# A written-out engine order for windowed attention and a two-layer block: uncast transposes for one pair, halved first-layer steps, and a new order of all steps

## The chip, the cores and the metric

The kernel runs on one core of one Trainium2 chip. The metric is device time in microseconds (us) from start to end of one execution. TensorE (PE in the profile) does the matrix products and transposes, VectorE (DVE) and ScalarE (ACT) empty PSUM and do the elementwise work, GpSimd (POOL) issues nearly all loads and does a few copies, SyncE (SP) issues stores, transposing DMAs and two loads. PSUM has eight banks, numbered 0 to 7.

## The reference

```python
B, H, S, D = q.shape                                   # 8, 8, 576, 64
scores = (1 / sqrt(D)) * q @ k^T                       # per batch and head
rel = pos[:, None] - pos[None, :]
scores = where((rel >= 0) & (rel < 64), scores, -1e9)  # causal window of 64
attn = softmax(scores)
x = (attn @ v).transpose(0, 2, 1, 3).reshape(4608, 512)
h = x @ w_in                                           # 512 -> 2048
out = (h - tanh(h)) @ w_out                            # 2048 -> 512, float32
```

## The kernel before

All products run on bf16 operands with float32 sums. The 4608 tokens are cut into nine chunks of 512 for the two dense layers; a batch has 576 tokens, nine windows of 64. The eight heads of a batch are handled in four pairs; pair g stands for batch g // 4, and pairs 0 to 3 are batch 0.

The whole kernel is one list of short words, `PLAN`, which `play` runs from left to right. Each word is a step (a small function) with its numbers and sometimes an engine (p POOL, a ACT, v DVE, s SP). There is no scheduler at run time: each engine does its own steps in the order of the words, waits for the data of each, and holds back everything behind it while it waits. The order of the words is therefore the order of every queue. The words that matter here:

- Loads. `lk.g`, `lq.g` load k and q of a pair (a cast to bf16 happens on the way when POOL issues them; pair 0 comes over SP as float32). `LV.b.i` loads v rows of a batch in blocks of 128 tokens (block 4 is the last 64), `lv.b.pr.half` and `lt.b` do the same by head and for the tail. `wi.i` (three) and `wo.i` (four) load the weights; `wi.2` is twice as large. `lr`, `qr` load k and q of batches 3 to 7, `tk`, `tq` transpose them by DMA.
- `ck.g`, `cq.g` copy a pair's rows into an order in which six transposes do (`tr`, L253). Without that copy `tr` takes twelve transposes of half the width straight from the loaded tile (L249). Before, pairs 2 and 3 do without; pairs 0, 1 and 4 to 11 have the copy.
- `Fp.g.bank`, `Ep.g.bank` are the transposes of k and q on PE; `Fc`, `Ec`, `Ea`, `Eb` move the result from PSUM to SBUF on the engine named.
- `Rp.g.part.bank` are the scores of a pair (for pairs 0 to 3 in two parts over two banks with the mask added by PE, L281 and L286; from pair 4 on in three parts of three matmuls, L292), `Rx` the exponentials on ACT, `M` the mask by product on DVE.
- `Z.b` (and `za`, `zb` by pair) copies v rows across partitions. `P.g`, `PP.g` are the products with v, `D`, `DS`, `DH`, `DR`, `DN` the division by the row sum on DVE into `xs`.
- `Xp.b.half.part.bank` transposes `xs` on PE, `Xc` moves it into `x_chunk`; half 0 holds pairs 0 and 1 of the batch, half 1 pairs 2 and 3. `Y` does the same by DMA for later batches.
- `H.c.m` is a first-layer step (`hp_mm`, L437: four matmuls of 512 columns, contraction 4 x 128), `A.c.m` its tanh on ACT (L445), `G.c.m` the subtraction on DVE (L451), `W.c.s.part` four of the sixteen matmuls of one output tile of the second layer (L480, and L473 for the last), `O` the copy out of PSUM and the store. For chunk 0 the steps H.0.m take the banks 0, 1, 2 in turn, so a step waits for the G of the step three places before it. Two of the four contraction slices of a step belong to half 0 and two to half 1 of `x_chunk`.
- `U.n` are n matmuls on a zero tile `warm` that feed nothing (L220); `i`, `h`, `n`, `u`, `mt`, `mq`, `mv`, `mk`, `mz` make constants and pads.

Of the kernel before, what the change touches and what calls it, by code (L numbers as in the profile page):

```python
# [15 lines left out]
def kernel(  # L16
# [491 lines left out]
    def subtract(c, m, s=None):
# [14 lines left out]
        H=first_layer, A=tanh, G=subtract, W=yp_mm, O=y_out)  # L523

    def play(script):
# [25 lines left out]
        Fc.9.3.a W.0.3.0 Rx.8.1.4 DN.6.0 DN.6.2 W.0.2.0 W.0.2.3 cq.10.a Rp.9.2.4 lr.3.2 Rx.9.2.4 LV.2.4 lr.4.0
        qr.3.3 W.0.3.1 Xp.1.1.0.3 qr.4.1 qr.3.1 Xc.1.1.0.3.a Rp.9.1.4 W.0.3.2 O.0.3.a W.0.2.2 M.8 Z.2 lr.3.4
        Xp.1.1.1.3 W.0.2.1 Xc.1.1.1.3.a LV.3.3 H.1.0 O.0.2.v Ep.10.3 A.1.0 Rx.9.1.4 tq.3.3 Eb.10.3.v H.1.1 H.1.2
        ck.11.v G.1.0 Ea.10.3.a Fp.10.3 Rp.9.0.4 A.1.1 H.1.3 A.1.2 qr.3.4 qr.3.0 lr.3.3 Fc.10.3.a lr.3.0 A.1.3
        qr.4.3 Rx.9.0.4 G.1.1 G.1.2 H.1.4 H.1.5 tq.3.0 qr.4.4 G.1.3 A.1.4 G.1.4 Fp.11.3 lr.3.1 lr.4.1 Rp.10.1.4
        mk M.9 A.1.5 Rx.10.1.4 cq.11.a H.1.6 H.1.7 G.1.5 Fc.11.3.a A.1.6 PP.8 G.1.6 DR.8 A.1.7 Rp.10.2.4 G.1.7
        Ep.11.3 Rx.10.2.4 Eb.11.3.a DN.8.0 LV.3.2 DN.8.2 H.1.8 A.1.8 Ea.11.3.a qr.3.2 LV.3.4 H.1.9 G.1.8
        Rp.10.0.4 H.1.10 Rx.10.0.4 A.1.9 Rp.11.1.4 Rx.11.1.4 tq.3.4 H.1.11 DN.8.1 G.1.9 LV.3.0 LV.3.1 A.1.10
        M.10 Rp.11.0.4 Xp.2.0.1.3 Rx.11.0.4 A.1.11 G.1.10 H.1.12 A.1.12 Rp.11.2.4 G.1.11 H.1.13 G.1.12 Rx.11.2.4
        M.11 H.1.14 A.1.13 A.1.14 PP.10 tk.3.1 Xc.2.0.1.3.v H.1.15 Xp.2.0.0.3 DR.10 A.1.15 G.1.13 tk.3.3 W.1.0.2  # L560
        Xc.2.0.0.3.a DN.10.2 DN.10.1 DN.10.0 tz.3.v G.1.14 W.1.0.1 tk.3.2 Xp.2.1.1.3 Xc.2.1.1.3.v W.1.0.0 G.1.15
        tq.3.2 tq.3.1 tk.3.0 tk.3.4 Xp.2.1.0.3 Xc.2.1.0.3.v W.1.0.3 H.2.1 O.1.0.v lr.5.1 H.2.0 lr.4.3 qr.5.4
        W.1.1.3 W.1.1.2 tq.4.3 A.2.1 G.2.1 A.2.0 qr.5.3 G.2.0 H.2.3 W.1.1.1 tk.4.1 A.2.3 LV.4.4 LV.4.2 G.2.3
        H.2.2 H.2.5 W.1.1.0 A.2.2 qr.4.2 A.2.5 G.2.2 LV.4.0 lr.4.4 O.1.1.a S.12 H.2.4 tk.4.3 G.2.5 Z.3 H.2.7
        LV.4.3 tq.4.1 Sx.12.0 A.2.4 Sx.12.2 G.2.4 A.2.7 W.1.2.2 H.2.6 qr.4.0 lr.4.2 W.1.2.0 W.1.2.3 M.12 qr.5.0
        LV.4.1 lr.5.0 Sx.12.1 M.13 G.2.7 PP.12 A.2.6 H.2.9 DR.12 G.2.6 W.1.2.1 A.2.9 DN.12.0 DN.12.2 O.1.2.a
        H.2.8 DN.12.1 G.2.9 S.14 H.2.11 A.2.8 tq.4.4 G.2.8 tq.4.2 H.2.10 W.1.3.3 W.1.3.0 Sx.14.0 Sx.14.2 M.14
        A.2.11 Sx.14.1 A.2.10 tk.4.4 G.2.11 M.15 G.2.10 tq.4.0 PP.14 H.2.13 tk.4.2 DR.14 DN.14.0 tk.4.0 A.2.13
        DN.14.1 H.2.12 lr.6.0 W.1.3.2 G.2.13 A.2.12 DN.14.2 Y.3 tk.5.0 G.2.12 H.2.15 W.1.3.1 tz.4.a H.2.14
        O.1.3.a A.2.15 W.2.0.2 W.2.0.0 A.2.14 G.2.15 G.2.14 LV.5.1 qr.5.2 qr.5.1 W.2.0.3 S.16 lr.5.2 W.2.0.1  # L570
        Sx.16.1 Sx.16.2 O.2.0.v H.3.0 Sx.16.0 LV.5.3 A.3.0 M.17 H.3.1 W.2.1.1 tq.5.2 lr.5.4 Z.4 M.16 G.3.0 A.3.1
        W.2.1.2 W.2.1.0 PP.16 LV.5.2 LV.5.0 G.3.1 LV.5.4 lr.5.3 H.3.2 DR.16 A.3.2 H.3.3 tq.5.0 DN.16.0 DN.16.2
        G.3.2 A.3.3 tq.5.4 G.3.3 DN.16.1 W.2.1.3 tq.5.1 lr.6.4 H.3.4 tk.5.1 A.3.4 O.2.1.v S.18 H.3.5 A.3.5 G.3.4
        W.2.2.0 H.3.6 G.3.5 Sx.18.1 Sx.18.2 M.19 H.3.7 A.3.6 W.2.2.3 G.3.6 A.3.7 Sx.18.0 H.3.8 W.2.2.2 G.3.7
        tk.5.4 M.18 H.3.9 A.3.8 G.3.8 A.3.9 G.3.9 W.2.2.1 O.2.2.v H.3.10 H.3.11 tk.6.0 tk.5.3 PP.18 A.3.11
        A.3.10 DR.18 DN.18.2 G.3.10 tk.5.2 W.2.3.3 tq.5.3 qr.6.3 G.3.11 W.2.3.1 DN.18.0 DN.18.1 H.3.12 A.3.12
        H.3.13 tz.5.v qr.7.3 W.2.3.2 G.3.12 Y.4 A.3.13 G.3.13 H.3.14 W.2.3.0 lr.6.1 H.3.15 O.2.3.a A.3.14 A.3.15
        Z.5 LV.6.1 W.3.0.2 G.3.15 G.3.14 W.3.0.1 qr.6.4 S.20 lr.6.2 qr.6.0 qr.6.1 H.4.0 H.4.1 Sx.20.0 A.4.0
        G.4.0 A.4.1 G.4.1 W.3.0.0 lr.7.3 H.4.2 lr.6.3 tk.6.1 H.4.3 A.4.2 G.4.2 W.3.0.3 Sx.20.2 A.4.3 Sx.20.1
        G.4.3 O.3.0.a tk.6.2 H.4.4 H.4.5 M.20 lr.7.2 A.4.4 qr.6.2 A.4.5 M.21 tq.6.4 G.4.5 PP.20 DR.20 DN.20.1  # L580
        tq.6.3 tq.6.1 LV.6.2 G.4.4 LV.6.3 LV.6.0 qr.7.4 DN.20.0 DN.20.2 W.3.1.2 W.3.1.0 H.4.7 W.3.1.3 W.3.1.1
        A.4.7 G.4.7 S.22 H.4.9 H.4.6 A.4.9 O.3.1.v A.4.6 Sx.22.2 tk.6.3 G.4.6 W.3.2.2 Sx.22.1 G.4.9 Sx.22.0 M.22
        M.23 W.3.2.0 W.3.2.1 W.3.2.3 H.4.8 tq.6.0 tk.6.4 tq.6.2 H.4.11 PP.22 A.4.8 G.4.8 A.4.11 O.3.2.a H.4.10
        LV.6.4 qr.7.0 W.3.3.0 tz.6.v DR.22 DN.22.2 G.4.11 H.4.13 LV.7.3 qr.7.1 W.3.3.1 LV.7.4 A.4.10 DN.22.0
        DN.22.1 W.3.3.2 LV.7.2 LV.7.1 W.3.3.3 G.4.10 A.4.13 H.4.12 G.4.13 A.4.12 Y.5 H.4.15 G.4.12 S.24 A.4.15
        H.4.14 Sx.24.2 A.4.14 O.3.3.v W.4.0.1 G.4.15 W.4.0.2 LV.7.0 G.4.14 W.4.0.3 Sx.24.1 lr.7.1 qr.7.2 Sx.24.0
        H.5.1 Z.6 M.24 A.5.1 M.25 W.4.0.0 O.4.0.v tk.7.2 H.5.0 lr.7.4 PP.24 G.5.1 A.5.0 H.5.3 G.5.0 DR.24
        W.4.1.1 A.5.3 tq.7.4 tk.7.3 tq.7.2 tq.7.1 tq.7.3 H.5.2 DN.24.0 W.4.1.3 lr.7.0 DN.24.1 DN.24.2 G.5.3
        A.5.2 G.5.2 W.4.1.2 H.5.5 A.5.5 G.5.5 H.5.4 S.26 A.5.4 H.5.7 tk.7.1 G.5.4 H.5.6 A.5.7 W.4.1.0 G.5.7
        Sx.26.2 A.5.6 H.5.9 Sx.26.1 G.5.6 O.4.1.v H.5.8 A.5.9 M.27 tk.7.4 W.4.2.3 A.5.8 Sx.26.0 G.5.8 W.4.2.1  # L590
# [50 lines left out]
```

## Time and profile before

| | |
|---|---|
| median of 3 runs | 312.04 us (312.03 to 312.27) |
| profiled execution | 311.42 us |
| its span, first to last instruction | 309.7 us |
| mean granted TensorE clock | 0.989 |
| PE busy | 301.3 us, 97% of the span |
| DVE, ACT, POOL busy | 183.7, 156.2, 103.0 us |
| HBM read, written | 36.70 MB, 9.44 MB |
| first H step starts | 27.93 us after the span's start |

Durations come from the profiled execution, and so sums are set against its 311.42 us; the runs without a profile lie 0.6 us above it. A matmul's recorded time includes the time in which it drains, so consecutive matmuls overlap in the records: what a group costs PE is the distance from its start to the next one's start.

### The profile page before, as it was taken

What the parts mean: (1) busy time and instruction counts of PE and PEld (TensorE: products, weight loads), DVE (VectorE), ACT (ScalarE), POOL (GpSimd) and SP (SyncE); (2) the same over time, 40 slices, a digit from 0 to 9 for tenths busy, and PEclk for the clock granted to TensorE, in tenths of its full rate; (3) what the DMA queues carried; (4) which work ended last, traced back from release to release, by engine and by line L of the source; (5) the groups of instructions that cost most, each with busy time, mean ns of one, the idle gap of its engine ahead of it and who ended that gap; (6) DMA issues with size and microseconds to landing.
All of it is one profiled execution on the core that took longest, in us unless ns stands there. A gap on an engine that the chain in (4) does not pass through costs nothing.

```text
span 309.7 us, 6275 instructions
## 1 busy us (share of the span) xinstructions
PE 301.3 (97%) x2522; PEld 159.8 (52%) x2522; DVE 183.7 (59%) x321; ACT 156.2 (50%) x266; POOL 103.0 (33%) x139
## 2 busy tenths in 40 slices
...
GB/s 151 132 176 199 197 182 187 181 169 141 145 137 162 148 117 151 164 155 125 159 160 177 161 179 117 89 134 35 3 70 110 34 35 34 34 34 36 37 65 102
DMA packets 133436, 37.33 MB, mean 121 GB/s; under 512 B 122016, under 2 KB 127904, under 8 KB 133408
## 3 DMA queue, kind: packets, MB, share of 16 engines
...
HBM read 36.70 MB, written 9.44 MB: 149 GB/s over the span
## 4 chain that ended last, share of the span: by engine, by line
PE 89%; DVE 3%; POOL 3%; DMA 2%; issue 1%; ACT 1%; POOLq 0%; ACTq 0%; DVEq 0%
PE ps L480 39%; PE ps L437 38%; PE ps L354 3%; PE ps L310 2%; DMA qall<-in_q_dram 2%; POOL vw L143 1%; PE ps L253 1%; DVE gT L451 1%; PE ps L473 1%; PE ps L292 1%; PE ps L403 1%; DVE qt L90 1%; PE ps L281 1%; POOL kall L108 1%; ACT th L445 1%
## 5 line engine op out<-in xcount | busy, mean ns | idle before, releaser
L451 DVE TENSOR_TENSOR gT<-ps,th 128x512 bf16<-128x512 f32 x144 | 97.7, 687 | 79.6 <-ACT th L445 79.0
L437 PE MATMUL ps<-xT,wi 128*128 128x512 bf16 x576 | 140.4, 380 | 0.5 <-DVE gT L451 0.2
L445 ACT ACTIVATE th<-ps 128x512 f32<-128x512 f32 x144 | 85.2, 598 | 100.0 <-PE ps L437 98.6
L480 PE MATMUL ps<-w_out_sb,gT 128*128 128x512 bf16 x560 | 134.3, 380 | 0.0
L437 PEld LDWEIGHTS <-wi 128*128 128x128 bf16 x576 | 63.0, 114 | 54.7 <-issue 0.9
L480 PEld LDWEIGHTS <-gT 128*128 128x128 bf16 x560 | 53.7, 98 | 60.9
L143 POOL DMA_DIRECT2D vw<-in_v_dram x35 | 30.5, 882 | 16.6 <-DVE q L90 9.0
L159 POOL DMA_DIRECT2D kall<-in_k_dram x25 | 21.6, 877 | 26.0 <-DMA kw<-kall 24.9
L159 POOL DMA_DIRECT2D qall<-in_q_dram x25 | 21.8, 879 | 20.9 <-DMA qw<-qall 17.5
L320 ACT ACTIVATE pt<-ps 128x1024 bf16<-128x1024 f32 (+1 forms) x30 | 23.3, 812 | 6.1 <-PE ps L310 5.9
L88 ACT ACTIVATE ysb<-ps 128x512 f32<-128x512 f32 (+1 forms) x20 | 11.6, 582 | 24.8 <-PE ps L480 19.7
L90 DVE COPY ysb<-ps 128x512 f32<-128x512 f32 (+1 forms) x17 | 11.6, 680 | 20.2 <-PE ps L480 19.5
L329 DVE TENSOR_TENSOR pt<-pt,ps 128x1152 bf16<-128x1152 bf16 x28 | 20.5, 746 | 3.2 <-ACT pt L320 2.8
L324 ACT ACTIVATE pt<-ps 128x384 bf16<-128x384 f32 (+2 forms) x32 | 16.9, 528 | 5.3 <-PE ps L292 3.4
L374 DVE TENSOR_TENSOR xs<-ps,rcp 128x384 bf16<-128x384 f32 x28 | 14.8, 550 | 0.2
L354 PEld LDWEIGHTS <-pt 128*64 128x64 bf16 x504 | 9.1, 111 | 5.1 <-issue 1.6
L354 PE MATMUL ps<-vw,pt 128*64 128x65 bf16 x504 | 10.7, 197 | 0.0
L220 PE MATMUL ps<-warm 128*128 128x512 bf16 x27 | 9.2, 498 | 1.1 <-DVE warm L197 1.1
L88 ACT ACTIVATE kt<-ps 128x576 bf16<-128x576 bf16 x10 | 6.5, 648 | 6.5 <-PE ps L253 3.5
L108 POOL DMA_DIRECT2D kall<-in_k_dram x11 | 7.3, 668 | 3.2 <-DMA wi<-in_moe_w_in_dram 1.8
L130 POOL DMA_DIRECT2D vw<-in_v_dram x8 | 6.7, 843 | 4.6 <-DMA wi<-in_moe_w_in_dram 4.5
L292 PE MATMUL ps<-qt,kt 128*128 128x128 bf16 x72 | 8.0, 219 | 0.0
...
## 6 DMA issues: line engine op xcount, KB each, us to landing
...
w_out_sb<-in_moe_w_out_dram POOLq DMA_DIRECT2D x4, 512.0 KB, 10.1
...
```

The costliest lines, as they stand in the source:

```text
L88: nc.scalar.activation(o, i, ACT.Copy)
L143: nc.gpsimd.dma_start(out=w[:, 2 * i + 1, :, 0:D] if i < NF else w[64:128, 2 * i, :, 0:D], in_=v[b, :, 128 * i:128 * i + n].rearrange("h p ...
L159: nc.gpsimd.dma_start(out=token_rows(b, n)[0:c, i], in_=(q if n == "q" else k)[b, :, 128 * i:128 * i + c].rearrange("h p d -> p h d"))
L320: nc.scalar.activation(o, sp, ACT.Exp, scale=scale)
L324: nc.scalar.activation(PT[g % NPT][:, js[0]:js[0] + len(js), :].rearrange("p i (h t) -> p i h t", h=2), sp, ACT.Exp, scale=scale)
L329: nc.vector.tensor_tensor(p, p, mask.unsqueeze(1).to_broadcast([128, 2 * NJ, 64]), ALU.mult)
L354: nc.tensor.matmul(ps[r, bank, 65 * i:65 * i + 65], PT[(g + r2) % NPT][:, j, r], vw[b % 2][:, j, p0 + r2 + NP * h, :], start=True, stop=True)
L374: nc.vector.tensor_tensor(xs[b % 2][:, 0:6, p0 + n // 2, :], ov[:, :, 0:D], sums[g][:, n].to_broadcast([128, 6, D]), ALU.mult)
L437: nc.tensor.matmul(hp, w_in_tile(ki, m), chunk_tile(c)[:, n.start // 64:n.stop // 64, ki % 2, 64 * (ki // 2):64 * (ki // 2) + 64], start=( ...
L445: nc.scalar.activation(th[:, n], hp, ACT.Tanh)
L451: nc.vector.tensor_tensor(gT[c][:, m, columns(s)], hp, th, ALU.subtract)
L480: nc.tensor.matmul(yp, gT[c][:, m, s * 128:(s + 1) * 128], w_out_sb[:, m, :], start=n == 1 and i == 0, stop=n == 4 and i == 3)
```

## The change

The work done is the same but for a few operations. Pair 1 loses `ck.1` and `cq.1`, so its two transposes become 24 narrow ones in place of 12 wide ones. The steps H.0.0, H.0.1 and H.0.2 become two calls each of `first_layer_part`, with the two contraction slices of one half of `x_chunk`; the six calls need not be neighbours. All other words occur as often as before, the 27 warm-up matmuls too. Their order is new from the first word to the last; many transposes and scores of batches 0 to 2 use other PSUM banks (3 to 7, and 0 to 2 in places, where before they nearly all used 3 and 4), and 44 of the 112 copies and casts named with an engine move between ACT and DVE.

```diff
@@ -502,6 +502,14 @@
     def first_layer(c, m, s=None):
         hidden[c, m, s] = hp_mm(c, m, s)
 
+    def first_layer_part(c, m, half):
+        n = turn("h", c, m)
+        hp = ps[:, m % 2 if c > 1 else (m + c) % 3, :]
+        for i in range(2):
+            nc.tensor.matmul(hp, w_in_tile(half + 2 * i, m), chunk_tile(c)[:, :, half, 64 * i:64 * i + 64],
+                             start=n == 1 and i == 0, stop=n == 2 and i == 1)
+        hidden[c, m, None] = hp
+
     def tanh(c, m, s=None):
...
-        H=first_layer, A=tanh, G=subtract, W=yp_mm, O=y_out)
+        H=first_layer, Hp=first_layer_part, A=tanh, G=subtract, W=yp_mm, O=y_out)
...
-        mt.1 mt.0 lk.1.p lq.1.p i u mv.0 LV.0.0 lk.5.p U.1 lk.0.s U.1 lq.0.s lq.3.p U.4 LV.0.3 LV.0.4 h LV.0.1
-        cq.0.a U.13 mq.0 mv.1 U.1.3 ck.1.a cq.1.v mq.1 Fp.1.2 Ep.1.3 LV.0.2 Fc.1.2.a U.2 ck.0.v Fp.0.2 lk.3.p
-        Ec.1.3.v Fc.0.2.v Rp.1.1.4 Ep.0.3 Ec.0.3.v Rx.1.1.4 lq.2.p Rp.1.0.0 lv.1.1.1 lk.2.p lq.5.p Rx.1.0.0 U.4
-        Rp.0.1.4 Rp.0.0.0 ck.5.a lk.4.p Z.0 Rx.0.1.4 Ep.3.3 Rx.0.0.0 Fp.3.2 lv.1.0.0 lk.6.p lq.4.p P.0 Fc.3.2.a
-        Ec.3.3.v lk.7.p D.0 Ep.2.3 Rp.3.1.4 Ec.2.3.a Rp.3.0.0 U.1.2 Rx.3.1.4 Fp.5.3 wi.0 Fp.2.2 cq.5.a Fc.5.3.v
-        P.1 lv.1.1.0 ck.4.v D.1 Rx.3.0.0 Fc.2.2.a Ep.5.3 Rp.2.1.4 Eb.5.3.a lq.7.p lv.1.0.1 wi.1 Rp.2.0.0
-        Rx.2.1.4 P.3 Rx.2.0.0 Ea.5.3.v wi.2 Fp.4.3 lq.6.p P.2 Xp.0.0.1.2 cq.4.v Fc.4.3.a Rp.5.0.4 D.3 DS.2
-        Xp.0.0.0.3 Rx.5.0.4 DH.2.0 Xc.0.0.1.2.a Xc.0.0.0.3.v DH.2.1 Xp.0.1.0.3 Xc.0.1.0.3.a Xp.0.1.1.2 Rp.5.1.4
-        Ep.4.3 Xc.0.1.1.2.v ck.6.v Ea.4.3.v Eb.4.3.v H.0.0 H.0.1 lv.1.2.0 A.0.0 Rx.5.1.4 lk.8.p cq.7.v lv.1.2.1
-        lq.8.p H.0.2 A.0.1 G.0.0 n lv.1.3.1 Rp.4.2.4 ck.7.v G.0.1 H.0.3 Rx.4.2.4 Rp.5.2.4 wo.0 A.0.3 Rx.5.2.4
-        G.0.3 Fp.7.3 H.0.4 Rp.4.0.4 A.0.2 N G.0.2 H.0.6 Rx.4.0.4 Fc.7.3.a M.5 A.0.4 za.1.0.v G.0.4 H.0.5 A.0.6
-        lv.1.3.0 Fp.6.3 Rp.4.1.4 A.0.5 Fc.6.3.a G.0.5 H.0.7 zb.1.0.p Ep.7.3 A.0.7 G.0.6 H.0.8 Ea.7.3.a G.0.7
-        cq.6.v A.0.8 H.0.9 Eb.7.3.v G.0.8 za.1.1.p Rx.4.1.4 H.0.10 A.0.9 zb.1.1.p lt.1 M.4 Rp.7.0.4 Ep.6.3
-        A.0.10 H.0.11 Eb.6.3.a Rx.7.0.4 G.0.9 wo.2 G.0.10 H.0.12 A.0.11 lq.9.p wo.1 Rp.7.2.4 Rx.7.2.4 H.0.13
-        wo.3 Ea.6.3.v G.0.11 A.0.12 cq.8.v lk.9.p Rp.6.1.4 H.0.14 G.0.12 Rx.6.1.4 Ep.8.3 ck.8.v H.0.15 A.0.14
-        Rp.6.2.4 lq.11.p LV.2.0 G.0.14 mz za.1.2.v lk.10.p Rx.6.2.4 PP.4 A.0.15 zb.1.3.p DR.4 Rp.6.0.4 DN.4.2
-        W.0.0.0 Ea.8.3.a LV.2.2 Eb.8.3.a za.1.3.v G.0.15 W.0.0.2 Rx.6.0.4 Fp.8.3 lq.10.p DN.4.1 cq.9.v Rp.7.1.4
-        W.0.1.2 W.0.1.0 Fc.8.3.a DN.4.0 zb.1.2.a M.6 Rx.7.1.4 M.7 Rp.8.0.4 Ep.9.3 Rx.8.0.4 A.0.13 PP.6 LV.2.1
-        Ea.9.3.a Eb.9.3.a W.0.0.1 Rp.8.2.4 W.0.1.1 Xp.1.0.0.3 Rx.8.2.4 DR.6 LV.2.3 G.0.13 W.0.1.3 Xc.1.0.0.3.a
...
-        W.7.2.1 G.8.10 H.8.12 G.8.9 W.7.2.3 A.8.12 W.7.2.0 H.8.11 O.7.2.a G.8.12 A.8.11 G.8.11 H.8.14 W.7.3.3
-        H.8.13 A.8.14 W.7.3.0 W.7.3.2 A.8.13 G.8.13 G.8.14 H.8.15 W.7.3.1 W.8.0.2 A.8.15 O.7.3.a G.8.15 W.8.0.1
-        W.8.3.3 W.8.0.0 W.8.0.3 O.8.0.v W.8.1.1 W.8.1.2 W.8.1.0 W.8.1.3 W.8.2.3 W.8.2.2 W.8.2.0 O.8.1.a W.8.2.1
-        W.8.3.2 O.8.2.v W.8.3.1 W.8.3.0 O.9.0.v O.8.3.a"""
+        u mv.0 lk.1.p i lq.1.p LV.0.1 lk.0.s lq.0.s lq.3.p lq.2.p LV.0.0 U.13 Fp.1.6 cq.0.v Ep.1.0 ck.0.v Fp.0.3
+        h lk.3.p Fc.1.6.v mt.1 lk.5.p mq.0 Fc.0.3.v mv.1 mt.0 U.4 Ec.1.0.a Rp.1.1.4 Rx.1.1.4 Rp.1.0.0 U.1.2
+        Ep.0.3 Ep.3.4 LV.0.2 U.4 Ec.3.4.v Fp.3.6 Ec.0.3.a Rp.0.1.4 Rx.1.0.0 LV.0.3 Rx.0.1.4 Rp.0.0.0 LV.0.4 U.2
+        Z.0 Fc.3.6.a Rp.3.1.4 Rx.3.1.4 Ep.2.2 U.1.3 Rx.0.0.0 lk.2.p lq.5.p lq.4.p P.1 Fp.2.7 Rp.3.0.0 D.1 P.0
+        cq.4.v ck.5.v lk.7.p Ec.2.2.a Fc.2.7.a D.0 Ep.4.3 Rp.2.1.4 Rx.3.0.0 Eb.4.3.a mq.1 lk.4.p Rp.2.0.0
+        Rx.2.1.4 Xp.0.0.1.2 lq.7.p wi.0 P.3 Xp.0.0.0.7 Rx.2.0.0 Xc.0.0.0.7.a cq.5.v ck.4.v Ep.5.4 P.2 D.3 DS.2
+        Eb.5.4.a DH.2.0 Fp.4.7 Fp.5.6 Fc.5.6.a Xp.0.1.0.0 U.1 DH.2.1 Xc.0.0.1.2.v Xc.0.1.0.0.a lq.6.p U.1
+        Xp.0.1.1.6 wi.1 lk.6.p Ea.4.3.a Hp.0.1.0 Ea.5.4.v Xc.0.1.1.6.v Hp.0.0.0 n wi.2 Fc.4.7.a Rp.5.2.3
+        Hp.0.0.1 ck.7.a A.0.0 Rp.4.1.5 Hp.0.1.1 Hp.0.2.1 lt.1 lk.8.p Hp.0.2.0 lv.1.0.1 Rp.4.0.6 Rp.5.0.7
+        lv.1.3.1 A.0.1 cq.6.v G.0.0 G.0.1 H.0.3 Rx.4.1.5 A.0.2 Rx.5.0.7 G.0.2 cq.7.v H.0.4 lv.1.0.0 Fp.7.4
+        Rp.5.1.2 Rp.4.2.5 A.0.3 G.0.3 A.0.4 Rx.4.0.6 Rx.5.1.2 Ep.7.7 N G.0.4 H.0.6 ck.6.v Eb.7.7.a Ea.7.7.v wo.2
+        H.0.5 A.0.6 G.0.6 H.0.7 Rx.5.2.3 Fp.6.3 A.0.5 lv.1.1.0 Rx.4.2.5 Ep.6.6 A.0.7 Fc.7.4.a H.0.9 G.0.5 H.0.8
+        Ea.6.6.a G.0.7 A.0.9 Eb.6.6.a A.0.8 lv.1.3.0 H.0.10 Fc.6.3.v G.0.9 ck.8.v wo.0 H.0.12 G.0.8 A.0.12
+        Rp.7.0.5 H.0.11 Rp.6.1.6 Rp.7.2.7 A.0.10 A.0.11 wo.1 G.0.12 G.0.11 zb.1.3.p Rp.6.2.3 Rp.7.1.4 H.0.15
+        Rx.7.0.5 Fp.8.5 H.0.14 za.1.0.v G.0.10 H.0.13 A.0.15 Rx.6.2.3 Rx.7.2.7 G.0.15 W.0.1.2 lv.1.1.1 W.0.1.0
+        M.4 mk lq.8.p zb.1.0.p wo.3 lv.1.2.0 lv.1.2.1 A.0.14 Rx.6.1.6 Rx.7.1.4 Rp.6.0.4 A.0.13 Rx.6.0.4 G.0.14
+        M.5 za.1.3.v Fc.8.5.v lq.10.p zb.1.1.p za.1.1.p lk.10.p W.0.0.0 lq.11.p lk.9.p W.0.0.2 W.0.0.1 cq.8.a
+        W.0.1.1 M.6 PP.4 G.0.13 Ep.8.3 W.0.1.3 lq.9.p DR.4 W.0.0.3 O.0.1.a Ea.8.3.v M.7 Eb.8.3.a DN.4.0 DN.4.2
+        zb.1.2.v O.0.0.a W.0.3.1 za.1.2.v DN.4.1 W.0.3.0 Rp.8.1.1 Rp.8.0.7 LV.2.2 lr.3.3 Rx.8.1.1 W.0.2.0
+        W.0.2.3 ck.9.v ck.10.v Rx.8.0.7 Xp.1.0.0.3 Rp.8.2.1 cq.10.a PP.6 W.0.2.2 Fp.9.4 DR.6 LV.2.0 DN.6.0
+        cq.9.a lk.11.p LV.2.1 Rx.8.2.1 Fc.9.4.a W.0.3.2 LV.2.3 Xc.1.0.0.3.v DN.6.2 DN.6.1 W.0.2.1 qr.3.3 LV.2.4
+        lr.3.1 qr.4.4 Xp.1.1.0.6 Xp.1.0.1.1 Xp.1.1.1.4 lr.3.2 Ep.10.7 Ep.9.3 Xc.1.1.0.6.v W.0.3.3 O.0.2.a qr.3.4
+        qr.3.0 Xc.1.1.1.4.v Xc.1.0.1.1.a Eb.9.3.a Eb.10.7.v M.8 Ea.10.7.v H.1.0 Ea.9.3.a Rp.9.0.3 O.0.3.a
+        Fp.10.4 H.1.1 Rx.9.0.3 Rp.9.2.6 A.1.0 G.1.0 H.1.2 A.1.1 Rx.9.2.6 ck.11.v tq.3.0 A.1.2 G.1.1 H.1.3
...
+        W.7.2.0 H.8.12 G.8.7 O.7.2.a A.8.12 H.8.11 A.8.11 W.7.3.1 W.7.3.3 G.8.11 G.8.12 H.8.13 W.7.3.0 A.8.13
+        G.8.13 H.8.14 A.8.14 H.8.15 A.8.15 G.8.14 W.7.3.2 O.7.3.a G.8.15 W.8.0.1 W.8.1.0 W.8.0.3 W.8.1.3 W.8.1.2
+        W.8.0.0 W.8.0.2 W.8.3.2 O.8.0.a W.8.2.0 W.8.2.1 W.8.1.1 W.8.2.3 O.8.1.a W.8.2.2 O.8.2.v W.8.3.3 W.8.3.0
+        W.8.3.1 O.9.0.a O.8.3.a"""
```

110 lines of the change are left out of this document (53 added, 57 removed).

## The prediction

> **What bounds the kernel now.** I read the page first, then stretches of the span, then the chain of waits, then the start engine by engine.
>
> ```profile
> PE 301.3 (97%) x2522; PEld 159.8 (52%) x2522; DVE 183.7 (59%) x321; ACT 156.2 (50%) x266; POOL 103.0 (33%) x139
> ...
> 13.08:16.49 3.41, 1.08 (x43) 0.82 (x36) 1.92 (x3) 1.24 (x2) 3.41 (x6) 1.00 1.41 173
> 16.49:19.90 3.41, 2.93 (x41) 1.42 (x36) 1.27 (x3) 1.89 (x4) 2.90 (x5) 0.50 1.43 179
> 19.90:23.32 3.42, 3.42 (x56) 2.55 (x55) 2.24 (x5) 2.06 (x5) 3.42 (x6) 0.50 1.19 173
> 23.32:27.93 4.61, 3.88 (x88) 3.10 (x87) 3.57 (x10) 3.60 (x7) 2.60 (x5) 1.00 1.42 190
> 30.53:46.62 16.09, 15.63 (x148) 9.50 (x147) 13.96 (x27) 12.72 (x25) 9.69 (x15) 1.00 1.28 191
> ...
> 249.50 0.86 PE ps L437 x4
> ```
>
> PE is the bound nearly everywhere: four matmuls of a first-layer step take 0.86 us and follow each other without a gap. So the end of the kernel moves with the moment at which PE has caught up with its work, and with stalls. The one poor place is the start. The second column of a stretch is its length, the next PE's busy time, the third from the end the granted clock: PE has 1.08 us of work in 3.41 us, and then runs for two such stretches, 6.83 us, at half clock.
>
> ```profile
> 10.45 0.61 POOL kall L108
> 11.05 5.96 DMA qall<-in_q_dram
> ...
> 27.53 0.56 DVE xT L90 x2
> ```
>
> ```profile
> 14.52 0.70 DVE L149 COPY vw<-vw 64x2080 bf16<-64x2080 bf16 x1 [3.37 <-DMA vw<-in_v_dram]
> 15.35 0.45 PE L249 MATMUL ps<-ident,kall 96*64 96x96 bf16 x12 [2.05 <-DMA kall<-in_k_dram]
> 27.93 2.75 PE L437 MATMUL ps<-xT,wi 128*128 128x512 bf16 x12
> ```
>
> The first fence is from the chain of waits (start, length, what), the second from the timeline (start, length, engine, line, how many, and in brackets the wait before). PE waits 2.05 us for k of pair 3. Batch 0's last needed input on the chain, q of pair 2, lands at 11.05 + 5.96 = 17.0, and H.0.0 starts at 27.93: 10.9 us of attention work, over half of it at half clock. The three steps H.0.0 to H.0.2 end at 27.93 + 3 x 0.86 = 30.5.
>
> **The loads, in the new order.** POOL issues one transfer after another, so a landing is a place in its queue.
>
> ```profile
> 8.65 1.79 POOL L143 DMA_DIRECT2D vw<-in_v_dram  x2
> DMA to landing us min/median/max: 4.7/5.0/6.5
> ```
>
> The first row is two issues of 0.9, the second of the v issues in the first 10.5 us; a k or q issue is the 0.61 of the chain above. Before, the last full v block is issued at 8.65 + 0.9 = 9.55. After, q of pair 2 and k of pair 3 stand ahead of it, and the tail block, which I price at 0.7, behind it: 9.55 + 2 x 0.61 - 0.7 = 10.1, landing at 15.1. `Z.0` ran from 14.52 until P.0 at 16.08 (below), 1.5 us, so it ends at 16.7 (before: 16.0). The tail block follows at 15.8 to 16.5, k of pair 2 at 16.8. So data of batch 0 is complete no earlier than before. But k of pair 3, issued at 10.45 before, has three v issues fewer ahead of it: out near 8.0, landed near 13.0. PE has transposes, U and scores of pair 1 until about 12.4, so it waits 0.6 us where it waited 2.05.
>
> **The chain from 16.7 to the first-layer steps.** In the new order DVE carries it. Prices:
>
> ```profile
> 16.08 0.51 PE L341 MATMUL ps<-vw,pt 128*64 128x65 bf16 x20 [0.28 <-DVE vw L150]
> 16.73 0.21 DVE L381 RECIPROCAL rc<-ps 128x10 f32<-128x10 f32 x1
> 16.97 0.82 DVE L383 TENSOR_TENSOR xs<-ps,rc 128x640 bf16<-128x640 f32 x1
> 7.16 0.38 DVE L90 COPY qb<-qall 96x768 bf16<-96x768 bf16 x1 [3.48 <-DMA qall<-in_q_dram]
> 7.61 0.54 DVE L207 MEMSET qt<- 128x576 uint32 x1
> 25.74 0.49 DVE L396 TENSOR_TENSOR xs<-ps,rc 128x320 bf16<-128x320 f32 x1
> 9.66 0.76 DVE L90 COPY kt<-ps 128x576 bf16<-128x576 bf16 x1 [0.21 <-PE ps L253]
> ```
>
> P.1 at 16.75 takes 0.51 and some 0.15 to be seen: D.1 starts at 17.4 and takes 0.21 + 0.82. Then `cq.4`, `ck.5` 0.76; D.0 1.03 (P.0 stands behind D.1 for its banks, 0.7 from D.1's end, so the casts are hidden); `mq.1`, `cq.5`, `ck.4` 1.30; D.3 1.03; DS.2 0.21; the two DH 0.98 at most; `Xc.0.0.1.2` 0.56; `Ea.5.4` 0.76; `Xc.0.1.1.6` 0.56. The sum is 8.2 us: half 0 of `x_chunk` is there at 24.3, half 1 at 25.6. PE's work fits beside it at full clock: in the same stretch before it was (2.93 + 3.42) / 2 + 3.88 = 7.1 us. The casts of pairs 4 and 5 wait for loads that are now nearer the front: q of pair 4 goes out two issues behind k of pair 2, at 13.0, and lands near 18.2, k of pair 4 two further, near 19.5, both before their turn (18.4 and 21.1); if not, D.0 and D.3 stand behind them.
>
> The halves: Hp.0.1.0 and Hp.0.0.0 run from 24.3, the other four from 25.6 on, with two score groups between: three steps are done at 27.5 in place of 30.5. Alone, halving is worth the 0.86 us that run before half 1 exists; it adds no columns. The casts of pair 1 removed (0.38 on DVE, the other on ACT) and twelve more transposes (0.45 in place of 0.42) lie in time in which PE waits for loads: nothing either way; without that cover 0.1 us for PE. `w_in` block 0 must have landed:
>
> ```profile
> 17.92 0.78 POOL L180 DMA_DIRECT2D wi<-in_moe_w_in_dram  x1
> 20.83 1.52 POOL L180 DMA_DIRECT2D wi<-in_moe_w_in_dram  x2
> DMA to landing us min/median/max: 7.4/8.8/13.1
> ```
>
> It landed at 17.92 + 7.4 = 25.4. The new queue has four half blocks of v fewer ahead of it; at 0.74 to issue (row further down) and less to carry I take 0.5 each, an estimate: 23.4. The third block landed 13.1 after its issue, at 21.6 + 13.1 = 34.7; with the same 2 us less and q of pair 6 more it comes near 33.3, just before H.0.9 (33.7).
>
> **First layer of chunk 0.** What a group costs PE is the distance to the next start:
>
> ```profile
> 42.30 0.33 PE L292 MATMUL ps<-qt,kt 128*128 128x128 bf16 x3
> 42.47 1.03 PE L437 MATMUL ps<-xT,wi 128*128 128x512 bf16 x4
> ...
> 44.36 0.42 PE L253 MATMUL ps<-ident,qb 96*128 96x96 bf16 x6
> 44.62 1.03 PE L437 MATMUL ps<-xT,wi 128*128 128x512 bf16 x4
> ...
> 51.27 0.70 PE ps L354 x36
> ```
>
> Before, the stretch 30.53 to 46.62 held 13 steps (11.2), nine score groups of 0.17 (1.5), five transpose groups of 0.25 (1.25), one PP (0.70, from the chain) and the mask: 14.8 of 16.09 us, so 1.3 us were lost with PE shown busy. DVE was busy for 13.96 of it.
>
> ```profile
> L451 DVE TENSOR_TENSOR gT<-ps,th 128x512 bf16<-128x512 f32 x144 | 97.7, 687 | 79.6 <-ACT th L445 79.0
> L445 ACT ACTIVATE th<-ps 128x512 f32<-128x512 f32 x144 | 85.2, 598 | 100.0 <-PE ps L437 98.6
> ```
>
> More banks free PE from waiting for one score bank, but a step still needs the G three places before it: tanh 0.60 and subtraction 0.69 behind the step. Walking the new order, most places have room; H.0.12 follows H.0.10 at once while ACT does Fc.7, Ea.6 and A.0.9 first, which costs 1.0, and H.0.11 0.2. I take the same 1.3 us as before; the bounds are 0 and twice that.
>
> **Second layer of chunk 0.** In the new order W.0.1.3 comes after 13 steps, ten score groups, PP.4, six transpose groups, the mask and six W groups: 20.4 us of PE work after 27.5, plus 1.3: 49.2. The same work took until 30.5 + 20.4 + 1.3 = 52.2 before. Its weights, `wo.3`, were issued second of these:
>
> ```profile
> 39.49 1.13 POOL L188 DMA_DIRECT2D w_out_sb<-in_moe_w_out_dram  x2
> DMA to landing us min/median/max: 9.1/10.1/11.0
> 34.91 0.74 POOL L130 DMA_DIRECT2D vw<-in_v_dram  x1 [4.46 <-DMA wi<-in_moe_w_in_dram]
> ```
>
> They landed at 40.1 + 11.0 = 51.1. Two half blocks of v and q of pair 9 move behind it (0.5, 0.5 and 0.7): 49.4 after, so 0.2 us of wait. The gain at this point is 2.8 us.
>
> **Everything later.** From chunk 1 on both orders keep at least two other steps between uses of a bank, and PE was without gaps, so I count nothing, bounds -0.5 and +0.5; the last words end both times with two narrow W groups behind which the store of the wide part hides. For waits that I have not seen I take off 0.2.
>
> **The sum.** 311.42 - 3.0 + 0.2 + 0.2 = 308.8 us for a profiled execution; the runs lie 0.62 above it (312.04 against 311.42), so 309.4 us.
>
> **A rule on the clock.** The row: 1.08 us of work in 3.41, with no wait above 2.05, was followed by half clock, and 2.93 of 3.41 busy did not lift it. By the gap of 0.6 us and my walk, PE stays above two thirds busy from 9.7 on, between these two rows, and I take full clock. The Trainium skill, "TensorE: Matmul & The Clock Gate", section "Why this matters for your kernels", wants no gaps above about 3 us; here 2.05 was enough, so the row decides. The Trainium skill says on the same page, in Part 4, that transposes do not count as busy in the same way. By that rule, which the row with 2.93 agrees with, the new start, with twelve more transposes, could fall to half clock: the first rival.
>
> **Rivals.** First, half clock all the same, from about 16.5 for two stretches. What PE's pieces then cost is in the trace:
>
> ```profile
> 21.09 0.75 PE L341 MATMUL ps<-vw,pt 128*64 128x65 bf16 x20
> ```
>
> 0.75 for 0.51. PE's 7.1 us become 10.4, while DVE's 8.2 go on beside it; where they alternate, neither hides the other. Price: 10.4 - 8.2 = 2.2, bounds 1 and 3.3. The time is 311.6. For it: the warm-up run is now 13 matmuls in place of 20, and PE again waits for loads. Against: the shorter gaps.
>
> Second, the gain is given back in chunk 0: PE arrives 3 us earlier, but tanh, exponentials and copies keep ACT and DVE at 80 to 90% in that stretch. Another 2.5 us lost there, twice what was lost before: 311.9. Against: the walk found room at all but two places.
>
> Third, slower: `wo.3` stands in POOL's queue behind the copies `zb.1.3` and `zb.1.0`, and the first waits for v that is itself loaded behind two blocks of `w_out`, near 40.2. Such a stop has been 4.46 us long. With two copies, two issues and it, `wo.3` goes out near 43.0; with the longest flight, 11.0, it lands at 54.0, PE stands 4.8 us at W.0.1.3, and all W, and H.1 after them, stand behind it: 313.2 + 0.6 = 313.8. It decides against the change once `wo.3` lands after 52.8. Against: fewer bytes are ahead of it than before.
>
> Fourth, the new order does what it says and no part of it matters, because batch 0's landing, which is not earlier, sets all: 312.0. Against: 6.83 us at half clock after the landing.
>
> **How the numbers follow.** Forecast 0.52; half clock 0.17; given back 0.08; `wo.3` late or loads late ahead of D.0 and D.3 0.18; nothing 0.05. A measurement of this kernel can tell about 0.2%, 0.62 us. Faster: the forecast and, since its price may be 1, part of half clock (0.12) and a little of the second, 0.66; same 0.14; slower 0.20. The forecast's own range is 308.3 to 310.6 (bounds of the first layer and of the rest). To leave out no more than 2 in 10 the range goes from 308.2 to 313.0.
>
> **What would show it.** In the profile after: no stretch at half clock between 7 and 300 us; PE waiting under 1 us for k; first L437 matmul near 24.3; three steps done at 27.5; W.0.1.3 near 49.3 and no wait for `w_out`; the stretch after it unchanged. Half clock after 16.5, an L437 start after 27, or a stop of PE before L480 would make it wrong, in this order of likelihood.

## The result, and the profile after

The changed kernel takes 324.74 us (median of four runs) beside 312.03 us before on the same chip. The ratio is 1.0376, 95% interval 1.0293 to 1.0459; this ratio and all later ones leave out executions in the chip's slow state, here the one of 328.93 us. The kernel is about 12 us slower, where 309.4 us was forecast. The profiled execution was the fastest of its runs, 321.31 us (span 319.5), so the trace shows some 3 us less of the loss than the median has.

The page of the changed kernel, busy tenths and granted clock in 40 slices of 8 us:

```profile
PE 302.6 (95%) x2534; PEld 159.6 (50%) x2534; DVE 182.5 (57%) x318; ACT 154.7 (48%) x267; POOL 102.7 (32%) x139
...
PE   8889999999999949999799969999999999999995
...
PEclk9979999999999998999999999999999999999999
```

PE has three holes, in the slices from 112, 152 and 184 us, all far behind the part that the prediction worked out. Stretches of 10 us around them (length, then PE's busy time; the clock is the third from the end) and PE's waits over the whole span:

```profile
110.00:120.00 10.00, 5.65 (x58) 2.83 (x57) 4.74 (x7) 2.90 (x5) 8.07 (x10) 0.98 1.92 124
120.00:130.00 10.00, 10.00 (x74) 4.69 (x73) 5.78 (x10) 4.57 (x8) 1.87 (x3) 0.85 1.56 130
150.00:160.00 10.00, 7.87 (x70) 4.07 (x69) 3.16 (x5) 4.62 (x9) 3.68 (x5) 1.00 1.90 173
180.00:190.00 10.00, 6.95 (x66) 3.59 (x65) 4.34 (x9) 3.09 (x5) 8.89 (x11) 1.00 1.45 103
```

```profile
PE ps L437 <- DMA xT<-xs: 9.5, 3, 4.3
PE ps L341 <- DVE vw L150: 2.0, 1, 2.0
...
119.23 2.12 PE L437 MATMUL ps<-xT,wi 128*128 128x512 bf16 x5 [4.35 <-DMA xT<-xs]
154.14 1.02 PE L437 MATMUL ps<-xT,wi 128*128 128x512 bf16 x4 [2.13 <-DMA xT<-xs]
189.35 1.89 PE L437 MATMUL ps<-xT,wi 128*128 128x512 bf16 x8 [3.05 <-DMA xT<-xs]
```

The first two lines sum the waits (us in all, how many, the longest); the others are from PE's timeline, with the wait in brackets. Three times a first-layer step waits for the chunk tile `xT` that a transposing DMA, a `Y` word, writes: 4.35 us at H.3.0, 2.13 at H.4.0, 3.05 at H.5.1, 9.5 in all. After the first wait the clock is 0.85 for 10 us, which is worth some 1.5 us more (an estimate, 0.15 x 10). The kernel before had no such wait. Set beside each other, step by step, PE's starts lie 2.66 us earlier than before at H.1.0 (61.55 against 64.21) and 9.30 later at W.8.3.0 (315.21 against 305.91).

Why Y came late is in the flights, a flight being the time from a transpose's issue to its landing. Each Y is two transposes: H.3.0 reads what the first part of Y.3 writes, and the second part belongs to the next chunk. The instructions of L422 (`x_dma`) between 109 and 117 us, Y.3's two parts; first the kernel before, then the changed one:

```profile
L422 SPq DMA_TRANSPOSE xT<-xs x2: 1366/1366/1367, 112.2 to 113.7; - x2
...
DMA to landing us min/median/max: 3.5/4.1/4.8
```

```profile
L422 SPq DMA_TRANSPOSE xT<-xs x2: 1763/2086/2408, 110.2 to 112.1; - x2
...
  PE ps L437: 4.3, 1
...
DMA to landing us min/median/max: 9.0/10.2/11.5
```

Y.3 left 2 us earlier than before (110.2 against 112.2), and its two parts landed 3.5 and 5.1 us later. What differs is GpSimd's queue at that time. The timeline of POOL, again before and after:

```profile
113.89 0.88 POOL L159 DMA_DIRECT2D kall<-in_k_dram  x1 [15.94 <-DMA kw<-kall]
114.76 0.88 POOL L143 DMA_DIRECT2D vw<-in_v_dram  x1
115.62 1.77 POOL L159 DMA_DIRECT2D qall<-in_q_dram  x2
```

```profile
109.58 3.12 POOL L159 DMA_DIRECT2D qall<-in_q_dram  x4 [11.22 <-DMA qw<-qall]
112.65 0.92 POOL L159 DMA_DIRECT2D kall<-in_k_dram  x1
113.53 2.01 POOL L143 DMA_DIRECT2D vw<-in_v_dram  x2
```

In both, GpSimd stands for more than 10 us at one load (in brackets), and the loads behind it leave in a burst when it is released. Before, the load at the head is lr.6.0. It needs tk.4.0, the last transpose of batch 4, to have read its buffer, so the burst left 1.7 us after Y.3's first part. In the new order qr.6.3 is at the head; it needs only tq.4.3, is released at 109.58, and ten loads leave from just ahead of Y.3's first part until it lands. At Y.4 it is the same with loads of batch 6: 8.51 and 11.84 us, before 3.23 and 6.10. Y.5 flew long in both (7.08 and 10.97, before 5.90 and 12.0).

Each wait is the flight of the first part less its lead, the time from its issue until PE reaches the step. In the changed kernel that is 8.98 - 4.68, 8.51 - 6.42 and 7.08 - 4.07 us. Before, the leads were 5.80, 4.44 and 9.09. With the flights of before (3.46 and 3.23) H.3.0 and H.4.0 would not have waited. At Y.5 the lead matters more than the flight: with the 5.90 us of before, H.5.1 would still wait 1.8.

### The profile page after: what moved, and what is told of

Same layout as the page of the kernel before. It is cut to its first block, busy times and chain, and to the rows that moved or that the text cites. A ratio compares the mean times of both kernels' runs of the same rounds, so it can differ in the third digit from the quotient of the medians.

```text
span 319.5 us, 6300 instructions
## 1 busy us (share of the span) xinstructions
PE 302.6 (95%) x2534; PEld 159.6 (50%) x2534; DVE 182.5 (57%) x318; ACT 154.7 (48%) x267; POOL 102.7 (32%) x139
## 4 chain that ended last, share of the span: by engine, by line
PE 73%; DMA 13%; DVE 5%; ACT 3%; POOL 2%; issue 2%; SPq 1%; POOLq 0%; ACTq 0%; DVEq 0%
PE ps L480 32%; PE ps L437 31%; DMA xT<-xs 5%; DMA vw<-in_v_dram 5%; PE ps L354 3%; DMA kw<-kall 2%; ACT th L445 1%; PE ps L310 1%; DVE gT L451 1%; PE ps L473 1%; PE ps L292 1%; PE ps L403 1%; POOL vw L143 1%; PE ps L509 1%; SPq L172 1%
## 5 line engine op out<-in xcount | busy, mean ns | idle before, releaser
L437 PE MATMUL ps<-xT,wi 128*128 128x512 bf16 x564 | 138.8, 383 | 9.8 <-DMA xT<-xs 9.5
L88 ACT ACTIVATE ysb<-ps 128x512 f32<-128x512 f32 (+2 forms) x24 | 13.9, 578 | 30.3 <-PE ps L480 27.4
L320 ACT ACTIVATE pt<-ps 128x1024 bf16<-128x1024 f32 (+1 forms) x30 | 23.1, 813 | 3.8 <-PE ps L310 3.6
L90 DVE COPY ysb<-ps 128x512 f32<-128x512 f32 x13 | 8.9, 688 | 18.8 <-PE ps L480 18.8
L324 ACT ACTIVATE pt<-ps 128x384 bf16<-128x384 f32 (+2 forms) x32 | 16.0, 535 | 5.4 <-PE ps L286 3.3
L374 DVE TENSOR_TENSOR xs<-ps,rcp 128x384 bf16<-128x384 f32 x28 | 15.0, 549 | 0.2
L371 DVE TENSOR_TENSOR xs<-ps,rcp 128x384 bf16<-128x384 f32 x14 | 7.7, 552 | 0.2
L149 DVE COPY vw<-vw 64x2080 bf16<-64x2080 bf16 x7 | 5.3, 759 | 4.3 <-DMA vw<-in_v_dram 4.2
```

The source lines that it names most:

```text
L88: nc.scalar.activation(o, i, ACT.Copy)
L320: nc.scalar.activation(o, sp, ACT.Exp, scale=scale)
L324: nc.scalar.activation(PT[g % NPT][:, js[0]:js[0] + len(js), :].rearrange("p i (h t) -> p i h t", h=2), sp, ACT.Exp, scale=scale)
L374: nc.vector.tensor_tensor(xs[b % 2][:, 0:6, p0 + n // 2, :], ov[:, :, 0:D], sums[g][:, n].to_broadcast([128, 6, D]), ALU.mult)
L437: nc.tensor.matmul(hp, w_in_tile(ki, m), chunk_tile(c)[:, n.start // 64:n.stop // 64, ki % 2, 64 * (ki // 2):64 * (ki // 2) + 64], start=( ...
```

## The experiments

Theory A: the loss is the burst of GpSimd loads that stands in flight beside Y.3, Y.4 and Y.5. Rival B: PE's place for H.3.0, H.4.0 and H.5.1 is too early, or Y's place too late, whatever flies beside it. Rival C: the loss comes from the new start. Rival D: SP's own transposes `tk` and `tq` lengthen Y's flights. Theory E, on the start, came up on the way: where PE has little to do ahead of P.1, half clock follows, and it costs the start its gain. Rival F: the gain goes for another reason. The runs are named e1 to e16.

Two aids recur. A hold is a copy of 64 elements per partition on GpSimd that reads what a Y wrote; it stands ahead of a load, so that load and all behind it leave when Y has landed. A fill is a number of `U` matmuls that feed nothing. In the short diffs a line of words is the order of `PLAN`. Each ratio is to runs of the kernel before on the same chip, whose median lay between 311.66 and 312.03 us.

**Which part of the order.** The two plans can be cut at H.1.4 and crossed.

```diff
 new start, old rest:  [changed plan up to H.1.4] + [what is left, in the order of before]
 old start, new rest:  [plan of before up to H.1.4] + [what is left, in the changed order]
```

> The changed kernel's words up to H.1.4 (its whole start, the halves and the uncast pair in it), and from there all words that are left in the order of the kernel before. Theory A (the loss is in the later order: a burst of GpSimd loads stands in flight beside the transposing DMAs Y.3, Y.4, Y.5 and makes them 2 to 3 times as long): the start keeps its 2.66 us at H.1.0 and no Y waits, so 312.0 - 2.6 = 309.4 us, 308.5 to 311.0; Y.3's two DMAs fly 3 to 5 us. Rival C (the loss belongs to the new start, which only shows later: products that reach chunk 3 earlier than its rows can be there): 318 to 322 us, with waits of 2 us or more for xT at H.3.0 and H.4.0. Rival B (PE's place for the first layer of chunks 3 to 5 is too early in the new order): as theory A, about 309.4 us.

> The other way round: the words of the kernel before up to H.1.4, then all that are left in the changed kernel's order. The part from H.1.0 on takes 321.3 - 61.55 = 259.8 us in the changed kernel and 312.0 - 64.2 = 247.8 us before. Theory A and rival B: 64.2 + 259.8 = 324.0 us, 321.5 to 326; H.3.0, H.4.0 and H.5.1 each wait 2 to 4 us for xT. Rival C: 311.5 to 313 us and no such waits.

New start, old rest (e1): 312.62 us (ratio 1.0022, 1.0001 to 1.0043). Old start, new rest (e2): 326.67 us (1.0448, 1.0387 to 1.0508), just above its range, with 8.8 us of waits for `xT` in three places. So the loss belongs to the later order, and rival C is out. The first kernel missed its 309.4, though. Its waits:

```profile
PE ps L341 <- DVE vw L150: 2.6, 1, 2.6
PE ps L305 <- DMA kw<-kall: 1.6, 1, 1.6
PE ps L437 <- DVE gT L451: 1.2, 1, 1.2
```

The second and third are seams of the cut (S.12 at 94.86, H.1.6 at 69.53). They take 2.8 us, more than the 2.4 that the start had gained in this trace (H.1.0 at 61.81 against 64.21). The first is in the new start itself, and comes back below.

**Is it the burst?** Hold the three bursts in the changed kernel; bring the burst forward in the kernel before.

```diff
+hold.3 qr.6.3 ...        +hold.4 LV.6.0 ...        +hold.5 LV.7.4 ...
 (in before)  ... LV.5.4 lr.5.3 +lr.6.0 ...   (and -lr.6.0 ahead of LV.5.1)
```

> The changed kernel with three small GpSimd copies that read what Y.3, Y.4 and Y.5 have written, put in GpSimd's queue ahead of the loads qr.6.3, LV.6.0 and LV.7.4, so that those loads and all behind them leave only once the Y has landed. Theory A: the flights of Y.3, Y.4 and Y.5 fall from 7 to 12 us to 3 to 6, the three waits at H.3.0, H.4.0 and H.5.1 (4.5, 2.3 and 3.2 us over the step before, 10.0 in all) go, and the time is 321.3 - 10.0 = 311.3 us, 310 to 314 if the held loads make something late. Rivals B and C: Y is as late as before and nothing is gained: 320 to 324 us. Rival D (Y's flight is long because of SP's own transposes tq and tk beside it): flights stay over 7 us, 320 to 324 us.

> The kernel before with one load moved: lr.6.0, which waits for the landing of tk.4.0 at 113.36 us and keeps ten loads of batch 5 behind it, goes behind lr.5.3, so that LV.5.1 and the loads after it can leave as soon as the products of batch 3 are done with V (PP.14, about 109 us), ahead of Y.3's issue at 112.2. Theory A: the burst now stands beside Y.3; its DMAs fly 8 us or more instead of 3.46 and 4.81, H.3.0 waits about 4 us for xT, and the time is 312.0 + 4 to 5 = 316.5 us, 314.5 to 318. Rivals B, C and D: Y.3's flights stay under 6 us, 312 us within 0.7.

With the three holds (e3): 313.65 us (1.007, 1.0039 to 1.0101), some 11 below the changed kernel's median; 0.6 us of waits for `xT` are left. Y.3's rows:

```profile
L424 SPq DMA_TRANSPOSE xT<-xs x2: 1357/1418/1480, 110.9 to 112.4; - x2
...
DMA to landing us min/median/max: 4.8/5.0/5.2
```

The kernel before with one load moved (e5): 319.12 us (1.0225, 1.0187 to 1.0262), and its rows:

```profile
L422 SPq DMA_TRANSPOSE xT<-xs x2: 2849/2962/3075, 112.7 to 115.6; - x2
...
  PE ps L437: 3.9, 1
...
DMA to landing us min/median/max: 10.6/10.7/10.9
```

One word moved makes the old kernel 7 us slower: 3.88 us at H.3.0, 1.31 us more at S.16 for k that tk.4.0 brings late, and a lower clock in the two slices that follow. The loss is thus taken away in one kernel and made in the other by the same thing, when the loads leave. The time is above the range of 314.5 to 318: the 4 to 5 us expected had counted neither the wait for k nor the clock.

**One burst alone.**

```diff
+hold.3 qr.6.3 ...        (hold.4 and hold.5 left out)
```

> The changed kernel with the hold at Y.3 alone (the copy ahead of qr.6.3); the bursts beside Y.4 and Y.5 are left. Theory A: the wait at H.3.0 (4.35 us, and about 1.5 us of lower clock behind it) goes, those at H.4.0 and H.5.1 stay within 1 us of 2.1 and 3.1: 321.3 - 6 = 315.3 us against the profiled run, 318 against the median of 324.7; 314.5 to 319. Rival B: the wait only moves to the next chunk, H.4.0 waits 5 us or more, and the time stays over 320.

322.65 us (e4; 1.0344, 1.0309 to 1.0379), outside what theory A said and inside what rival B said. The wait at H.3.0 is 0.68 us, but the next has grown from 2.13:

```profile
155.17 1.86 PE L439 MATMUL ps<-xT,wi 128*128 128x512 bf16 x4 [6.01 <-DMA xT<-xs]
```

The trace says why this is not a matter of PE's place. PE reaches H.4.0 2.9 us earlier than in the changed kernel (149.2 against 152.0), and Y.4's first part now flies 10.45 us instead of 8.51 and lands 1.0 us later: the held loads of batch 5 run into those of batch 6, and eight loads are in flight at its issue where six were. With all three held, Y.4's first part flies 5.09 us, and H.4.0 does not wait although PE reaches it at 147.1. The three waits don't add up: each Y lands when the loads beside it let it, and time won ahead of it is waited away there.

**How many loads.** Ten loads beside Y.3 are left out, then only the last five of them.

```diff
-qr.6.3 -qr.5.0 -qr.6.4 -qr.5.4 -lr.5.3 -LV.5.4 -LV.5.1 -lr.6.3 -qr.5.1 -lr.5.4
```

> The changed kernel without the ten GpSimd loads that leave beside Y.3 (qr.6.3, qr.5.0, qr.6.4, qr.5.4, lr.5.3, LV.5.4, LV.5.1, lr.6.3, qr.5.1, lr.5.4; batch 5 and part of 6 are then computed from older rows). Theory A: Y.3's two DMAs fly 3 to 5 us instead of 8.98 and 11.50 and H.3.0's wait of 4.35 us is under 0.5. Rival D (own transposes or Y's place): flights over 7 us and a wait over 3 us remain.

> As the kernel with ten loads left out, but only the last five of them (LV.5.4, LV.5.1, lr.6.3, qr.5.1, lr.5.4) are left out; qr.6.3, qr.5.0, qr.6.4, qr.5.4 and lr.5.3 stay. Theory A, flights in proportion to the bytes beside them: half way between, 5 to 8 us, with a wait of 0.5 to 3 us at H.3.0. If it takes only one load in flight to slow Y down: as in the changed kernel, 9 to 11.5 us; if there is a threshold above five: under 5 us.

315.83 (e15) and 320.44 us (e16), one run each. Ten left out, then five left out:

```profile
  PE ps L437: 0.5, 1
...
DMA to landing us min/median/max: 4.6/4.9/5.2
```

```profile
  PE ps L437: 1.9, 1
...
DMA to landing us min/median/max: 5.8/6.1/6.5
```

With ten, five and no loads Y.3's first part flies 8.98, 6.48 and 5.17 us, and with the same lead of 4.68 H.3.0 waits 4.35, 1.85 and 0.54. (Without loads the flight and the wait lie just over what was expected.) More loads make it longer. Number and distance in time are not separated, though: in these two traces the start ran late, so that Y.3 left at 112.80 and 113.13 instead of 110.20, and the five loads left up to 4.5 us ahead of it, while in the changed kernel one left 0.6 us ahead and the others behind. Own transposes (rival D) were there in all three, the last of them 4.4 to 4.8 us ahead of Y.3, so rival D is out.

Rival B keeps a share at the third place. In e15 the loads beside Y.5 are untouched; its first part flies 5.79 us, no longer than before, and H.5.1 still waits 1.76, since the lead is 4.07 and not 9.09. The holds take that wait away too, by bringing the flight down to 2.73.

**A seam further on, and what the start is worth.** The changed plan is kept up to W.2.0.1, behind Y.3, with the old order and a hold from there. On it, two parts of the change are undone one at a time.

```diff
 e6: [changed plan up to W.2.0.1] lr.5.1 qr.5.4 qr.5.3 qr.5.0 +hold.3 lr.6.0 [rest as before]
 e7: e6 with Hp.0.m.0 and Hp.0.m.1 replaced by one H.0.m
 e8: e6 with +ck.1.a ahead of Fp.1.6 and +cq.1.v ahead of Ep.1.0
```

> The changed kernel's order up to W.2.0.1, behind Y.3, and from there the words that are left in the order of the kernel before, with the hold ahead of lr.6.0 so that the burst leaves when Y.3 has landed. Both waits at the seam of the first mixed kernel (1.19 us at H.1.6, 1.59 us at S.12) should be gone. Theory A: the start's gain of 2.2 to 2.4 us comes through to the end: 309.4 us beside 311.7 to 312.0 of before, 308.6 to 310.6; no wait for xT over 0.6 us. If the start's gain is always given back by something later, whatever the order: 311.5 to 313 us.

> As the second kernel of this call, but with the first three first-layer steps of chunk 0 whole (H.0.0, H.0.1, H.0.2 at the place of their second halves). The copy that the second half needs ends at 26.5 us, the first half could start at 25.55; only Rp.5.2.3 (0.17 us) is left to fill that. If the halves do what they are for, this kernel is 0.4 to 0.9 us slower than the second one; if they only move work that would wait elsewhere, within 0.2 us of it.

> As the second kernel of this call, but pair 1 of batch 0 is cast before it is transposed, k on ScalarE and q on VectorE, as in the kernel before. In the changed kernel the products P.1 wait until 17.31 us for VectorE's copy of V (Z.0), so pair 1 has slack: 0 to 0.5 us slower if that wait covers it, 0.8 us or more if VectorE's cast pushes Z.0 or the first copies, and up to 0.5 us faster if the plain transposes were the longer way (they need 36 matmuls where the cast ones need 12).

e6: 312.2 us (0.999, 0.996 to 1.0021). No wait for `xT`, no seam, and still nothing gained; in its trace 1.1 us are left of the gain at H.1.0 and 0.1 at H.5.1. e7: 311.81 us (1.0001, 0.9971 to 1.0032), not to be told from e6. e8, with the casts that the change had removed: 310.12 us (0.9941, 0.9918 to 0.9964), 2 us better than e6, by the ratios 1.5. That is better than any of its three expected outcomes (and the uncast transposes need 24 matmuls, not 36). PE at P.1, and stretches around it, in e6:

```profile
18.11 0.76 PE L343 MATMUL ps<-vw,pt 128*64 128x65 bf16 x20 [3.01 <-DVE vw L152]
```

```profile
14.00:18.00 4.00, 1.10 (x23) 0.58 (x21) 1.43 (x2) 1.74 (x3) 2.35 (x4) 0.90 1.34 167
18.00:25.00 7.00, 6.89 (x127) 4.74 (x127) 4.42 (x12) 3.39 (x6) 5.64 (x11) 0.57 1.15 172
```

and in e8:

```profile
17.25 0.51 PE L343 MATMUL ps<-vw,pt 128*64 128x65 bf16 x20 [1.46 <-DVE vw L152]
```

```profile
14.00:18.00 4.00, 2.48 (x58) 1.58 (x59) 1.62 (x3) 2.28 (x5) 3.12 (x5) 1.00 1.34 171
18.00:25.00 7.00, 6.35 (x142) 4.73 (x141) 6.51 (x17) 5.76 (x10) 5.69 (x11) 1.00 1.23 197
```

P.1 waits for V in both. In e6 PE has run out of work at 15.1 and stands 3.01 us; then 7 us run at a clock of 0.57. In e8 the casts hold pair 1 back, PE has work until 15.8, the hole (the time in which PE stands) is 1.46, and the clock stays full. Of the 1.55 between them 0.86 is V, which came earlier in this execution (P.1 at 17.25), and 0.7 the casts: a cheaper pair 1 made the hole longer. Over the runs: of e6's twelve, nine had a mean clock of 0.988 or 0.989 (311.6 to 313.7 us) and two 0.999 (309.4); none of e8's was under 0.994.

**Is it the hole?** Fill it and leave all else.

```diff
 e9:  e6 with +U.9 ahead of P.1          e11: e10 with whole H.0.0, H.0.1, H.0.2
 e10: e8 with +U.6 ahead of P.1          e12: before with +U.8 ahead of Fp.3.2
```

> The mixed kernel with the hold (new order to W.2.0.1, then the old one) and nine idle products (128 by 512, 0.21 us each, 1.9 us) in TensorE's queue ahead of P.1, where TensorE had nothing to do for 2 to 3 us. Theory E: the idle time there (TensorE busy for 1.10 us of the 4 from 14 to 18) is what halves the clock afterwards, for about 6 us in most runs, at a cost of about 3 us; with it filled the clock stays full and the start's gain of 2.2 to 2.4 us is there in most runs: 309.4 us, 308.5 to 310.3, 2 to 3 us faster than without the fill. Rival F (the gain is lost by late landings of V or by something else, and the clock follows from another cause): within 0.5 us of 312.2.

> The same with pair 1's casts back (which measured 310.1 us without a fill) and six idle products, 1.3 us, ahead of P.1. Theory E: TensorE was already busy for 2.48 of the 4 us from 14 to 18 and its clock was full in the profile, so the fill only takes away the runs that lost part of it: 309.4 us, 308.7 to 310.1. If the casts themselves and not TensorE's busy time were what helped: also 310, and then e9 stays near 312.

> As the second kernel of this call with the first three first-layer steps whole. With the clock held by the fill, the halves can be read alone: if they are worth what the trace says, 0.4 to 0.9 us slower than the second kernel; if nothing, within 0.3 us.

> The kernel before with eight idle products, 1.7 us, ahead of Fp.3.2, where TensorE waited 2.05 us for k of pair 3 and the clock was halved from 16.5 to 23.3 us. Theory E: the half clock goes; work of about 6 us was done at half rate, which costs 3 us, of which some hides waits: 310.2 us, 309.3 to 311. Rival F: within 0.5 us of 312.0.

e9 310.26 us (0.9952, 0.9933 to 0.997), e10 309.87 (0.9955, 0.9933 to 0.9977), e11 311.29 (0.9988, 0.9961 to 1.0014), e12 311.14 (0.9975, 0.9955 to 0.9996). e9:

```profile
14.00:18.00 4.00, 2.90 (x30) 1.31 (x23) 1.17 (x2) 1.74 (x3) 2.05 (x4) 1.00 1.39 164
18.00:25.00 7.00, 5.99 (x161) 4.64 (x160) 5.84 (x15) 4.66 (x8) 5.92 (x11) 1.00 1.15 172
```

e6 and e9 ran on different chips. Set against the kernel before on its own chip, e9 is 1.7 us better than e6 by the medians and 1.2 by the ratios, whose intervals touch. The clock is plainer: none of e9's nine runs was under 0.993, and P.1 came no earlier (18.37). So nine matmuls that compute nothing keep the clock up and are worth 1 to 2 us; theory E holds, and rival F's 312.2 is out. Eight such matmuls help the kernel before too, by 0.7 us, which is short of theory E's range and more than rival F's. In its trace 1.3 us are won at H.1.0 (62.91 against 64.21) and 0.2 are left at H.5.1 (178.65 against 178.89); where the rest goes is not shown. The halves can't be settled: e11 is 1.4 us slower than e10, e7 0.4 faster than e6, both within the spread. e8, e9 and e10 are faster than both kernels, by 0.5 to 0.6% against before, and not to be told from each other.

**Both causes out of the changed kernel.**

```diff
 e13: changed kernel with +U.9 ahead of P.1     e14: that with hold.3, hold.4, hold.5
```

> The changed kernel with nine idle products ahead of P.1 and nothing else. Theory E (idle TensorE ahead of P.1 halves the clock for some 4 to 6 us) with theory A: the start is 1.5 to 2.5 us earlier in most runs, but the loads' bursts set when Y.3, Y.4 and Y.5 land, and the waits for xT take half or more of it: 324.7 falls to 322.5 to 324. If the waits take none of it: 322. If they take all: 324.7.

> The changed kernel's own order with the three holds and the nine idle products: both causes taken away. 313.65 (three holds alone) less 2.0 (what the fill brought the mixed kernel) = 311.6 us, 310.6 to 312.6; waits for xT under 0.7 us, full clock. If a third cause of more than a microsecond is left in the new order: over 313.

e13 323.28 us (1.0393, 1.0324 to 1.0463), in the expected range, though its few runs lie too far apart to say which share of the fill's gain the Y waits take. Its trace reaches H.1.0 no earlier than the changed kernel's (61.66 against 61.55), but V came 1.15 us later there (P.1 at 18.46 against 17.31). e14 312.12 us (1.0007, 0.998 to 1.0034), as before and within its bounds; of the waits for `xT` 0.4 us are left. Each set against before on its own chip, it is 1.7 us behind e9, which has the old rest; no single wait in its trace is that long, and what else the new rest costs stays open.

## Why the prediction was wrong

**The step that failed** is "Everything later": "I count nothing, bounds -0.5 and +0.5". It measured +12.0 us in the profile (from 2.66 us ahead at H.1.0 to 9.30 behind at W.8.3.0), and 15.0 in the runs with the old start (326.67 against 311.66). The reason given was banks and a PE without gaps; GpSimd's queue and the Y transposes of the new order were not walked, although the prediction walked the same queue for every load of the start. In its place the runs showed transposes that fly 7 to 9 us beside a burst of loads, against leads of 4.1 to 6.4 us: 9.5 us of waits in three places, and a lower clock behind the first. No rival held this. In the plan it could be seen: qr.6.3 and nine loads stand behind Y.3, with tq.4.3 as the only thing that holds them, and Y.5 stands 4.1 us ahead of H.5.1 where it stood 9.1.

**Full clock** was the second step to fail. The first rival, half clock from about 16.5 at 311.6 us, is what e6 shows without the Y waits: 312.2. The profile of the changed kernel has it too, for a shorter time (mean clock 0.82 from 18 to 25 us), and there it cost little:

```profile
17.31 0.77 PE L341 MATMUL ps<-vw,pt 128*64 128x65 bf16 x20 [2.01 <-DVE vw L150]
```

The wait for k of pair 3 did shrink, from 2.05 us to 0.19 (0.6 forecast), but the hole moved on to P.1, which the walk had given no wait at all. Seven traces with a hole of 2.0 to 2.9 us in the start had half clock behind it. The Trainium skill, "TensorE: Matmul & The Clock Gate", section "Why this matters for your kernels", asks for no gap above about 3 us between bursts of matmuls; that is too lax here. e9 has the twelve added transposes and full clock. What the Trainium skill says in Part 4 of that page, that transposes do not count as busy in the same way, is not needed to explain it.

**The start otherwise** came close.

```profile
15.76 0.70 DVE L149 COPY vw<-vw 64x2080 bf16<-64x2080 bf16 x1 [4.15 <-DMA vw<-in_v_dram]
16.46 0.79 DVE L150 COPY vw<-vw 64x2080 bf16<-64x2080 bf16 x1
```

```profile
25.55 1.03 PE L509 MATMUL ps<-xT,wi 128*128 128x512 bf16 x4
```

Z.0 ended at 17.25 (16.7 forecast), the first half step began at 25.55 (24.3), the three steps were done at 28.48 (27.5), W.0.1.3 began at 49.84 (49.2); wi.0 landed at 23.1 (23.4), wo.3 at 49.0 (49.4). The third rival, `wo.3` late, did not occur; the most that any run lost there was 0.8 us, in e10. The gain forecast was 3.0 us behind the three steps and 2.8 at W.0.1.3; the trace has 2.05 behind the steps (28.48 against 30.53) and 2.66 at H.1.0, so the second rival, the gain given back in chunk 0, did not occur either. But the gain hangs on how long the hole is in a run: with the hole as e6's trace has it, 1.1 us are left at H.1.0.

**The halves** were priced at 0.86 us alone; no pair of runs shows it or excludes it. **Pair 1 without casts** was counted at nothing "either way", with 0.1 us of PE as the price if the cover goes. The cover was priced from the wrong side: less work for PE in a stretch where it waits lengthens the hole. e8 against e6 puts that at 1.5 to 2 us, and with the hole filled (e10 against e9) it is 0.4, within the spread.
